# A fused attention and expert kernel: two more units take the two-level Strassen second product

## Chip, cores and metric

The kernel runs on one core of one Trainium2 chip. The metric is the device time of one execution in microseconds. The kernel before took a median of 1163.72 us in three runs (1161.91 to 1165.33).

A core has five engines that run side by side, each through its own instruction list in order: PE (matrix multiply), DVE (VectorE), ACT (ScalarE), POOL (GpSimd), and SP (SyncE), which here does nothing but issue transfers between DRAM and on-chip memory. An instruction that needs data from another engine, or a buffer that another still holds, waits on a semaphore at the head of its engine's list, and everything behind it in that list waits too.

## The reference

```
# 1. linear attention with decay, blocks of 64 positions
for b in range(nb):
    intra = ((qb @ kb.T) * Dmask) @ vb
    out[b] = intra + (qb * lam_pow) @ kv_state
    kv_state = lam_block * kv_state + (kb * rev_pow).T @ vb
# 2. bridge: (B,H,S,D) -> x of 3072 tokens x 512
# 3. mixture of 4 experts
p = probs / (probs.sum(-1) + 1e-9)
out = sum(p[:, e:e+1] * (relu(x @ w1[e]) @ w2[e]) for e in range(4))
```

There are 4 sequences, 8 heads, 768 positions and a head size of 64. Each w1[e] is 512 x 1024, each w2[e] is 1024 x 512. All is float32.

## The kernel before, in words

The 3072 tokens are cut into three groups of 1024 (g = 0, 1, 2). A **unit** is one group with one expert (g, e), so there are twelve; the list `units` has them in the order of the work. While the second product (h @ w2) of unit number `at` runs, the first product (x @ w1) of unit `at + 1` runs beside it, instruction by instruction.

**Strassen.** One Strassen level makes a product of 2 x 2 blocks with seven block products M1 to M7 instead of eight; its operands are blocks (A11, A12, A22) and sums of blocks (S1 to S4 of one factor, T1 to T4 of the other). The first product uses two levels in every unit: seven outer products, each of seven inner ones (`first_product`, matmuls in line 1017). The second product comes in two forms. Units 0 to `NEST - 1` use one level (`second_product`, line 1071): seven products, each summed into the tokens' accumulators and weighted with the gate by DVE (lines 1085 and 1089). Units from `NEST` on use two levels (`nested_product`, line 1370), and here `NEST` is 6: 4 operands of the outer level on the token side are made by DVE (`outer_sums`), 4 inner sums for each outer product by POOL (`inner_sums`, four 128 x 512 subtractions), the gate is multiplied onto the hidden values by POOL before the product (`gated`), and the result is collected in seven `sums` tiles, which occupy all seven buffers of the pool `stage`.

**Operands of w2.** The one-level form reads w2 blocks and the sums T1 to T4 of them (`prepare_w2`, stored in `w2_sums` in DRAM). The two-level form reads 49 operands for each expert, which POOL makes and SP stores in `w2_ops` in DRAM (`prepare_w2_ops`): blocks of w2 are loaded, four outer sums S1 to S4 are made (two 128 x 512 subtractions each), and for each of M1 to M7 four inner sums (four 128 x 256 subtractions) are made and stored in six transfers. The form called with `eased=True` uses tiles of the general pool `small` (42 buffers) instead of `stage`. The same kind of chain makes the operands of w1 (`prepare_w1`, stored in `w1_ops`).

**What sets the order of the work.** The order is written out by the Python code. A product is eight **slots** long; `now` counts slots. At the end of every slot `pump` may issue one preparation step from the list `chores`, if a count of the work given to POOL (`busy`) says that POOL is not behind. Finished sums are stored through `queue`, some slots later. Whoever needs an operand calls `until`, which, if the operand's store has not been issued, issues chores and stores one after another, at once, until it has been: `feed` (w1 operands, tile `ws_in`, line 930, two buffers, issued for the next product), `feed2` (one-level w2 operands, tile `w2t`, line 1052, two products ahead), `feed3` (two-level w2 operands, tile `w2t`, line 1129, six buffers shared with `feed2`; the first tile for a unit is fed in slot 1 of the last product before it). Gates, inner sums and DVE's work go through the lists `aside`, `background` and `lately`, one step a slot. All transfers named here are issued by SP, in the order of the code.

**Attention** of the groups 1 and 2 is woven into the units: `attention(g)` gives each of eight token blocks its load, transposes, scores and values at fixed slots, `BEGIN[g] = (first slot, slots from block to block)`. For each pair of blocks POOL makes block sums (`pair_sums`). `x_fill` loads the finished x of the group (tile `xs`) and POOL or DVE makes its inner sums.

**Before**, group 1 runs experts 0, 1 with one level and 2, 3 with two, and its one-level result goes through a DRAM buffer `partial` and is added at the end (`gather`, `finish_rows`). The w2 operands of experts 2 and 3 are made during units 4 and 5, those of experts 0 and 1 from unit 6 on, and the attention of group 2 runs from slot 152 to slot 276 (a unit has 56 slots).

Of the kernel before, what the change touches and what calls it, by code (L numbers as in the profile page):

```python
# [21 lines left out]
def kernel(  # L22
# [99 lines left out]
    units = [(g, e) for g in range(NG) for e in ((2, 3, 0, 1) if g == LAST else range(E))]  # L122
    unit_of = {u: x for x, u in enumerate(units)}
    NEST = 2 * E - 2
# [414 lines left out]
    gate_bc = decay[:]  # L539
# [240 lines left out]
    def pair_sums(g, x, o):  # L780

        s = stage.tile([P, 4, 256], FP32, name="to", tag="st")
        (b12, b11), (b22, b21) = ((t[:, 0:256], t[:, 256:512]) for t in o)
        for to, a, b in ((0, b12, b11), (1, b22, s[:, 0]), (2, b22, b12), (3, b21, s[:, 1])):
            tt(nc.gpsimd, s[:, to], a, b, ALU.subtract)
# [3 lines left out]
            nc.sync.dma_start(out=x_blocks[g - 1, :, x, 3:7], in_=s[:]),  # L789
# [4 lines left out]
    BEGIN = {1: (24, 13), 2: (8 * 19, 16)}  # L794
    steps = []

    def attention(g):
# [3 lines left out]

        for i in range(CPG):
            n, s = g * CPG + i, BEGIN[g][0] + BEGIN[g][1] * i
            put(s - 10, lambda n=n: load_more(n))
            put(s - 6, lambda n=n: load(n, "v"))
            put(s, lambda n=n: turn(n, ("s0", "s1")))
            if comes_across(n):
                put(s - 2, lambda n=n: (decayed(n), nat.pop((n, "k"))))
            put(s + (6 if comes_across(n) else 4), lambda n=n: scores(n, ("s0", "s1")))
            put(s + (12 if comes_across(n) else 10), lambda n=n: values(n, ("s0", "s1")))  # L810
            if n == NG * CPG - 1:
                put(s + 17, turn_gates)
        steps.sort(key=lambda s: s[0])

    def forget():
        while lately:
            take(lately, True)
        assert not states
# [38 lines left out]
    def gated(e, i, j, at, t):  # L857

        def step():
            n = j * 4 + (int(at[1]) - 1) * 2  # L860
            x = t[:].rearrange("p (c t) -> p c t", c=2)
            by = gate_bc[:, n:n + 2].rearrange("p n t -> p (n t)").unsqueeze(1).to_broadcast([P, 2, 256])
# [7 lines left out]
    def outer_sums(e, *names):  # L870
# [5 lines left out]
        def bring(x, at, tag):  # L876
# [3 lines left out]
            there[x] = bank(tag, "hp")  # L880
            nc.scalar.copy(out=there[x][:], in_=blk[at][:])  # L881

        def total(name, at):
            a, b = of[name]
            o = small("h" + name)
            tt(nc.vector, o[:], there[a][:], outer[e][b][at][:], ALU.subtract)
# [54 lines left out]
    def finished(g, e, m, blocks, new):  # L941

        def later(to, a, b, order, relu=False):
# [7 lines left out]
            def step(at):  # L951
                x = there[at]
                if unit_of[g, e] >= NEST and at != order[-1]:
# [11 lines left out]
            if unit_of[g, e] >= NEST:  # L965
# [90 lines left out]
    def second_product(g, e, m, banks):  # L1056

        def part(sj, s):
# [31 lines left out]
            if unit_of[g, e] in (E - 1, NEST - 1) and m in ("M2", "M6", "M5", "M3"):  # L1090
                to = rows[n] if g == 0 else partial[n % CPG * P:(n % CPG + 1) * P]
# [12 lines left out]
    partial = dram.tile([G, DOUT], FP32, name="partial")  # L1104
# [185 lines left out]
    def first_result():  # L1290
# [19 lines left out]
        def gather(n):  # L1310
            t, po = small("y"), small("po")
# [6 lines left out]
            nc.sync.dma_start(out=po[:], in_=partial[n * P:(n + 1) * P])  # L1318
            gathered_out[n] = t, po

        def turn_rows(n):
            t = gathered_out[n][0]
# [3 lines left out]
        def finish_rows(n):  # L1326
            t, po = gathered_out.pop(n)
            tt(nc.gpsimd, t[:], t[:], po[:], ALU.add)
            store(lambda: nc.sync.dma_start(out=rows[CPG + n], in_=t[:]))
# [296 lines left out]
    for g in range(1, NG):  # L1626
        attention(g)
    PACE = 1.0, 1.4, 1.0
    first_steps = first_result()
    PREPARED = {NEST - 2: (2, 3), NEST: (0, 1)}  # L1630
    for at, (g, e) in enumerate(units):
        if at == 0:
            chores.extend(prepare_w2(2) + prepare_w1(3) + prepare_w2(3) + prepare_w1(0))
        ahead = units[at + 1] if at + 1 < len(units) else None
        nested, nests = at >= NEST, ahead and at + 1 >= NEST
        if at in PREPARED:
            for x in PREPARED[at]:
                chores.extend(prepare_w2_ops(x, nested))
        if at == NEST:
            spare.append(True)  # L1640
        if at == NEST - 1:
            forget()
        blocks, banks = {}, {}
        for i in range(7):
# [8 lines left out]
            if nests and i == 2:  # L1653
                nc.scalar.dma_start(
                    out=gate_bc, in_=gate_rows[ahead[0] - 1, :, ahead[1]].partition_broadcast(P),
                )
# [24 lines left out]
            for x, part in enumerate(order):  # L1681
# [8 lines left out]
                elif (ahead or x % 2 == 0 and x + i) and not (nests and i == 6 and x == 7):  # L1690
                    if nested or nests:
                        rest()
# [60 lines left out]
```

## Time and profile before

| | |
|---|---|
| median of three runs | 1163.72 us |
| profiled execution, first to last instruction (span) | 1164.6 us |
| its own time as a run | not listed apart from the span |
| PE busy | 1149.6 us (99%) |
| POOL busy | 748.3 us (64%) |
| DVE busy | 810.8 us (70%) |
| ACT busy | 306.2 us (26%) |
| granted PE clock, mean | 0.998 |

In the page's groups a line such as `L1071 PE MATMUL q<-w2t,m` gives line, engine, operation, what is written and read, and then the number, the busy time and the mean time of one. One float32 matmul of the code leaves two records. Neighbouring matmuls overlap, so busy time divided by count, not the mean, is what one costs. A table of windows gives, for each stretch of the span, the busy time of each engine with its number of instructions, the granted PE clock, the share of busy transfer engines and the rate. The lines themselves are shown in the prediction.

### The profile page before, as it was taken

What the parts mean: (1) busy time and instruction counts of PE and PEld (TensorE: products, weight loads), DVE (VectorE), ACT (ScalarE), POOL (GpSimd) and SP (SyncE); (2) the same over time, 40 slices, a digit from 0 to 9 for tenths busy, and PEclk for the clock granted to TensorE, in tenths of its full rate; (3) what the DMA queues carried; (4) which work ended last, traced back from release to release, by engine and by line L of the source; (5) the groups of instructions that cost most, each with busy time, mean ns of one, the idle gap of its engine ahead of it and who ended that gap; (6) DMA issues with size and microseconds to landing.
All of it is one profiled execution on the core that took longest, in us unless ns stands there. A gap on an engine that the chain in (4) does not pass through costs nothing.

```text
span 1164.6 us, 21683 instructions
## 1 busy us (share of the span) xinstructions
PE 1149.6 (99%) x8039; PEld 997.4 (86%) x8039; DVE 810.8 (70%) x1483; ACT 306.2 (26%) x618; POOL 748.3 (64%) x720
## 2 busy tenths in 40 slices
PE   8899999999999999999999999999999999999998
PEld 7788888888888888888888888888888888888887
DVE  4576896477478757747946775688875677777785
ACT  4312122112201211221221243342343341341232
POOL 2747427456754862243646395897995898995894
PEclk9999999999999999999999999999999999999999
DMA  8883668999999797787969557676668877876542
GB/s 191 213 277 119 182 190 255 311 297 284 314 301 298 258 315 204 205 261 240 291 204 281 187 190 227 213 225 216 212 222 261 244 230 227 277 225 212 172 190 73
DMA packets 291705, 270.63 MB, mean 232 GB/s; under 512 B 139600, under 2 KB 239504, under 8 KB 291600
## 3 DMA queue, kind: packets, MB, share of 16 engines
q1 hardware_dynamic: 278848, 265.36, 74.1%
q10 hardware_dynamic: 12752, 3.89, 1.5%
q8 instruction: 64, 1.05, 0.4%
q14 instruction: 41, 0.34, 0.1%
HBM read 191.55 MB, written 81.82 MB: 235 GB/s over the span
## 4 chain that ended last, share of the span: by engine, by line
PE 93%; DVE 4%; DMA 1%; issue 1%; ACT 0%; ACTq 0%; DVEq 0%
PE pg L1017 39%; PE q L1071 24%; PE pq L1370 19%; PE pM L1473 3%; PE pc L1473 2%; DVE m L102 2%; PE sp L676 1%; PE op L730 1%; DMA ws_in<-w_ops 1%; PE op L748 1%; PE sp L683 1%; DVE sums L102 1%; PE qp L646 1%; PE kp L646 1%; DVE hT L102 0%
## 5 line engine op out<-in xcount | busy, mean ns | idle before, releaser
L1017 PE MATMUL pg<-xs,ws_in 128*128 128x256 f32 x1960 | 472.0, 381 | 2.3 <-DMA ws_in<-w_ops 1.2
L1017 PEld LDWEIGHTS pg<-xs,ws_in 128*128 128x128 f32 x1960 | 369.5, 190 | 56.5 <-DVE m L102 4.6
L102 DVE TENSOR_TENSOR m<-pg,m 128x512 f32<-128x512 f32 x451 | 307.1, 687 | 124.6 <-PE pg L1017 112.8
L1071 PE MATMUL q<-w2t,m 128*128 128x256 f32 x1344 | 318.7, 380 | 0.5 <-DVE m L102 0.5
L1071 PEld LDWEIGHTS q<-w2t,m 128*128 128x128 f32 x1344 | 254.1, 190 | 35.8 <-DVE m L102 1.2
L102 POOL TENSOR_TENSOR m<-m,decay 128x512 f32<-128x512 f32 x96 | 121.0, 1282 | 75.2 <-ACT m L1029 58.0
L1029 ACT ACTIVATE m<-m 128x512 f32<-128x512 f32 x132 | 83.0, 630 | 244.4 <-DVE m L102 241.0
L1370 PE MATMUL pq<-acc,w2t 128*128 128x256 f32 x576 | 141.9, 379 | 0.2 <-DVE sums L102 0.2
L102 DVE TENSOR_TENSOR sums<-pq,sums 128x256 f32<-128x256 f32 x223 | 92.7, 421 | 59.2 <-PE pq L1370 47.8
L1089 DVE SCALAR_TENSOR_TENSOR acc<-q,gate,acc 128x256 f32<-128x256 f32 x136 | 65.4, 481 | 87.5 <-PE q L1071 86.6
L1370 PEld LDWEIGHTS pq<-acc,w2t 128*128 128x128 f32 x576 | 109.2, 190 | 15.7 <-POOL w2o L102 0.5
L102 DVE TENSOR_TENSOR m<-m,m 128x512 f32<-128x512 f32 x136 | 112.9, 830 | 4.2 <-ACT m L1029 4.2
L1025 ACT COPY m<-pg 128x512 f32<-128x512 f32 x88 | 51.5, 585 | 161.7 <-PE pg L1017 158.7
L102 POOL TENSOR_TENSOR acc<-hT,acc 128x512 f32<-128x512 f32 x48 | 61.3, 1276 | 5.2 <-PE pq L1370 1.8
L102 POOL TENSOR_TENSOR to<-xc 128x256 f32<-128x256 f32 x16 | 12.6, 785 | 79.6 <-DVE xc L102 47.1
L102 POOL TENSOR_TENSOR acc<-hT,hT 128x512 f32<-128x512 f32 x48 | 60.7, 1282 | 3.9 <-PE pq L1370 3.9
L1370 PE MATMUL pq<-hT,w2t 128*128 128x256 f32 x240 | 61.6, 379 | 0.0
L102 POOL TENSOR_TENSOR xs<-xs 128x256 f32<-128x256 f32 x40 | 30.4, 761 | 47.0 <-DMA xs<-x_blocks 33.3
L102 POOL TENSOR_TENSOR kn<-kn,decay 128x512 f32<-128x512 f32 x16 | 18.1, 1133 | 63.2 <-PE kp L646 27.6
L949 ACT COPY up<-m 128x512 f32<-128x512 f32 x48 | 27.8, 589 | 101.6 <-DVE m L102 101.4
L881 ACT COPY hp<-m 128x512 f32<-128x512 f32 x72 | 41.6, 589 | 37.5 <-DVE hT L102 20.3
L1370 PEld LDWEIGHTS pq<-hT,w2t 128*128 128x128 f32 x240 | 45.6, 190 | 6.2
(140 smaller groups left out, 1371.0 us busy)
## 6 DMA issues: line engine op xcount, KB each, us to landing
ws_in<-w_ops SPq DMA_DIRECT2D x70, 896.0 KB, 6.9
w2t<-w_ops SPq DMA_DIRECT2D x108, 256.0 KB, 3.7
w2b<-in_moe_w_dram SPq DMA_DIRECT2D x56, 256.0 KB, 6.1
w_ops<-ops SPq DMA_DIRECT2D x28, 512.0 KB, 4.7
w2t<-w_sums SPq DMA_DIRECT2D x48, 256.0 KB, 3.7
w2t<-in_moe_w_dram SPq DMA_DIRECT2D x36, 256.0 KB, 3.9
w_sums<-w2o SPq DMA_DIRECT2D x16, 512.0 KB, 5.4
xs<-x_blocks SPq DMA_DIRECT2D x28, 256.0 KB, 4.5
```

What stands on the lines that cost most here:

```text
L102: eng.tensor_tensor(out=o, in0=a, in1=b, op=op)
L646: nc.tensor.transpose(out=x[:, ac * C:(ac + 1) * C], in_=y[:, 2 * ac:2 * ac + 2].rearrange("p r d -> p (r d)"), identity=ident[:],)
L676: nc.tensor.matmul(out=sp[r][half[x], ac * BL:(ac + 1) * BL], lhsT=hc(kT)[half[r], ac, blk[x]], rhs=hc(qT)[half[r], ac, blk[x]], start=(ac ...
L881: nc.scalar.copy(out=there[x][:], in_=blk[at][:])
L949: nc.scalar.copy(out=there[at][:], in_=a[at][:])
L1017: nc.tensor.matmul(out=p[:, j * 256:(j + 1) * 256], lhsT=ws[i][:, j * P:(j + 1) * P], rhs=xs[i], start=(fresh and j == 0), stop=True, skip ...
L1025: nc.scalar.copy(out=new[at][:], in_=p[:])
L1029: nc.scalar.activation(out=new[at][:], in_=new[at][:], func=AF.Relu)
L1071: nc.tensor.matmul(out=p[:, s * DH:(s + 1) * DH], lhsT=h[A_OF[m]][:, c * 256 + s * P:c * 256 + (s + 1) * P], rhs=fed2[g, e, m][uu][:, c], ...
L1089: nc.vector.scalar_tensor_tensor(out=o, in0=x, scalar=w, in1=o, op0=ALU.mult, op1=ALU.add)
L1370: nc.tensor.matmul(out=p[:, 0:256], lhsT=fed3[e, m, x // 2][:, x % 2, c * P:(c + 1) * P], rhs=b[B_OF[i]][:, c * 256:(c + 1) * 256], start= ...
L1473: nc.tensor.matmul(out=p[:, s * 256:(s + 1) * 256], lhsT=a[c][:, f:f + P], rhs=b[:, c, j * 256:(j + 1) * 256], start=(s == 0 and c == 0 an ...
```

## The change

`NEST` becomes 4, so units 4 and 5 use the two-level form too; group 1 now runs its experts in the order 2, 3, 0, 1, like group 2. The buffer `partial` and its addition are gone. The two-level operands of w2 for experts 2 and 3 are made by chores of the units 0 to 3; whatever is left of `chores` when unit 4 begins is issued there at once. Those of experts 0 and 1 are listed as chores at the start of unit 4. The attention of group 2 starts at slot 128 with 13 slots from block to block and ends in unit 4. Each two-level unit gets its own pair of gate tiles (`spread_gates`) in place of the shared one. In unit 4 the outer sums and some additions read on-chip tiles directly, without the copy to PSUM that later units use (`unit_of[g, e] > NEST`).

```diff
-    units = [(g, e) for g in range(NG) for e in ((2, 3, 0, 1) if g == LAST else range(E))]
+    units = [(g, e) for g in range(NG) for e in ((2, 3, 0, 1) if g else range(E))]
...
-    NEST = 2 * E - 2
+    NEST = E
...
+    def spread_gates(g, e):
+        gate_bc[unit_of[g, e]] = two = [small("gb")[:].rearrange("p (n t) -> p n t", t=P) for _ in range(2)]
+        for j, t in enumerate(two):
+            src = gate_rows[g - 1, 4 * j:4 * j + 4, e]
+            nc.scalar.dma_start(out=t, in_=src.partition_broadcast(P))
...
-        s = stage.tile([P, 4, 256], FP32, name="to", tag="st")
+        s = [small("to") for _ in range(2)]
...
-    BEGIN = {1: (24, 13), 2: (8 * 19, 16)}
+    BEGIN = {1: (24, 13), 2: (24 + 8 * 13, 13)}
...
+        def idle(slot):
+            return ("s0", "s1") if slot < NEST * 56 else (("q11", "q12"), ("q01", "q02"))[slot // 8 % 2]
...
-            there[x] = bank(tag, "hp")
-            nc.scalar.copy(out=there[x][:], in_=blk[at][:])
+            if e > NEST:
+                there[x] = bank(tag, "hp")
+                nc.scalar.copy(out=there[x][:], in_=blk[at][:])
...
-            t, po = gathered_out.pop(n)
-            tt(nc.gpsimd, t[:], t[:], po[:], ALU.add)
-            store(lambda: nc.sync.dma_start(out=rows[CPG + n], in_=t[:]))
+            t = gathered_out.pop(n)
+            nc.sync.dma_start(out=rows[CPG + n], in_=t[:])
...
-    PREPARED = {NEST - 2: (2, 3), NEST: (0, 1)}
...
-            chores.extend(prepare_w2(2) + prepare_w1(3) + prepare_w2(3) + prepare_w1(0))
+            chores.extend(
+                prepare_w2(2) + prepare_w1(3) + prepare_w2_ops(2, False) + prepare_w2(3) + prepare_w2_ops(3, False)
+                + prepare_w1(0)
+            )
...
-        if at in PREPARED:
-            for x in PREPARED[at]:
-                chores.extend(prepare_w2_ops(x, nested))
         if at == NEST:
+            while chores:
+                print("forced")
+                pump(force=True)
+            for x in (0, 1):
+                chores.extend(prepare_w2_ops(x, True))
             spare.append(True)
...
-                nc.scalar.dma_start(
-                    out=gate_bc, in_=gate_rows[ahead[0] - 1, :, ahead[1]].partition_broadcast(P),
-                )
+                spread_gates(*ahead)
```

## Prediction

> **What bounds the kernel now.** I read the page's busy times first, then a table of windows by unit, then what one instruction and one transfer cost, and last the piece of the chain where PE once had to wait. From the page:
>
> ```profile
> span 1164.6 us, 21683 instructions
> PE 1149.6 (99%) x8039; PEld 997.4 (86%) x8039; DVE 810.8 (70%) x1483; ACT 306.2 (26%) x618; POOL 748.3 (64%) x720
> ```
>
> PE is busy almost throughout, so a matmul less shortens the run, provided that nothing makes PE wait. The windows (window; busy us and instructions of PE, PEld, DVE, ACT, POOL; clock; transfer share; GB/s) show a start-up stretch, unit 4 (one level, attention beside it), unit 5 (one level), and units 7 to 10 (two levels); the bounds are where the second product's line or unit changes in the timeline.
>
> ```profile
> 44.00:48.00 4.00, 3.95 (x62) 3.78 (x62) 2.30 (x4) 0.92 (x2) 3.62 (x4) 0.57 0.76 233
> 495.00:594.60 99.60, 99.60 (x838) 86.32 (x836) 70.37 (x126) 17.82 (x40) 45.43 (x52) 1.00 0.85 258
> 594.60:686.30 91.70, 91.15 (x422) 79.55 (x421) 59.14 (x94) 21.91 (x38) 55.32 (x54) 1.00 0.66 207
> 767.20:850.90 83.70, 83.61 (x388) 73.16 (x387) 70.57 (x129) 27.52 (x49) 73.01 (x65) 1.00 0.71 222
> 850.90:935.60 84.70, 82.88 (x379) 71.29 (x378) 54.15 (x94) 35.99 (x75) 67.17 (x60) 1.00 0.77 241
> 935.60:1017.30 81.70, 81.70 (x379) 71.72 (x378) 61.28 (x113) 25.20 (x45) 74.12 (x70) 1.00 0.80 244
> 1017.30:1099.90 82.60, 82.60 (x384) 72.55 (x384) 61.38 (x115) 24.42 (x43) 64.00 (x53) 1.00 0.70 213
> ```
>
> Seen here: a one-level unit takes 91.7 us, 99.6 with attention; a two-level one takes 83.2 (mean of four), 11.9 per outer product, 1.49 per slot. POOL is at 64 to 74 us of such a unit: near its limit, but PE doesn't wait, because the preparation is spread evenly. Prices, from the groups and the transfer list (the last figure is us to landing):
>
> ```profile
> L102 POOL TENSOR_TENSOR acc<-hT,hT 128x512 f32<-128x512 f32 x48 | 60.7, 1282 | 3.9 <-PE pq L1370 3.9
> L102 POOL TENSOR_TENSOR ops<-w2o 128x256 f32<-128x256 f32 x28 | 20.7, 760 | 0.2
> ...
> ws_in<-w_ops SPq DMA_DIRECT2D x70, 896.0 KB, 6.9
> w2t<-w_ops SPq DMA_DIRECT2D x108, 256.0 KB, 3.7
> w2b<-in_moe_w_dram SPq DMA_DIRECT2D x56, 256.0 KB, 6.1
> w_ops<-ops SPq DMA_DIRECT2D x28, 512.0 KB, 4.7
> ...
> L315 SPq DMA_DIRECT2D w_ops<-ops x84: 319/496/2052, 513.3 to 1052.6; - x84
> ```
>
> So POOL takes 1.28 us for a 128x512 subtraction and 0.76 for a 128x256 one; issuing a transfer holds SP 0.5 us. Last, the chain:
>
> ```profile
> 883.80 1.51 PE pg L1017 x7
> 885.31 11.68 DMA ws_in<-w_ops
> 896.99 0.14 issue
> 897.13 1.97 PE pg L1017 x8
> ```
>
> The first product's weights are issued about one product (11.9 us) ahead and arrive just in time. Whatever holds SP for longer stops PE.
>
> **The change part by part.**
>
> *Gain.* 91.7 - 83.2 = 8.5 us a unit, 17 for two. Counted otherwise: 28 records fewer a unit, at 318.7/1344 = 0.237 us, 13.3 for two. I take 15.
>
> *Added POOL work, by count.* 32 more gate products and 56 more inner subtractions, 8 additions fewer: 80 x 1.28 = 102 us. In all, 748 + 102 = 850 of some 1150 us fits. What matters is when it comes. The order that the changed code builds shows four places where chores are not spread but issued together, because a reader forces them or because unit 4 begins. After unit 4's start the count of POOL's work is 40 slots ahead, so `pump` issues nothing until unit 5 ends; the operands for experts 0 and 1 are then made only when `feed3` asks.
>
> *A, start of unit 4.* In the last four products of unit 3 POOL is given 16.3, 12.3, 21.0 and 15.4 us of work (instructions by the rows) against 99.6/7 = 14.2 us each, so it is 8.1 late. Then eleven steps of expert 0's w1 chain stand at once in POOL's and SP's lists; SP gets to the `w2t` loads of unit 4's first product only behind the store of the tenth. Ten steps: six times 4 x 0.76 and four times 2 x 1.28, 28.5 us, and 3 for block A12, whose load (7.8 us to landing, w1b 512 KB) stands behind the third store. 8.1 + 31.5 + 3 issues 1.5 + load 3.7 = 44.8. PE needs the tile in slot 4 with some scores before it, 6.5 us in. Stall 38. Without lateness and A12: 27; with 12 of lateness and 5 of waits for the seven `stage` buffers: 48.
>
> *B, expert 0's operands.* In slot 1 of unit 5's last product ten steps are forced. One gate product and four leftover block sums of attention hold POOL, and SP behind them, for 4.6 us; two stores and four loads issue (3.0); landing 6.1: 13.7. S1 2.6, four sums for M4 3.0, S3 2.6, four for M7 3.0, four for M1 3.0: 27.9. Six stores issue (3.0), then the first `w2t` can load, its pieces having landed by 32.6: 36.3. Due after 7 slots, 10.4: stall 26. `ws_in` issues behind it at 33.6 and lands at 40.5, while PE has 1.5 us to do: 3 more. In the next product M3's operands are forced: after M1 POOL has M5 (3.0), nine 128x512 (11.5), then S2, M6, M2, S4, M3 (14.2), done at 56.6; landing 4.7, load 3.7 and issues 1.5: 66.5. PE is through at 40.5 + 10.4 = 50.9: stall 15.6, and 2.5 again for `ws_in`. B = 47; from 30 (stores and loads half hidden) to 55.
>
> *C, expert 1's, one unit later.* The same without block sums and first loads, but behind twelve sums of x (9.1): M1 ready on POOL at 1.3 + 9.1 + 14.2 = 24.6 in place of 27.9. C = 47 - 3.3, rounded 43; from 27 to 52.
>
> *D, units 2 to 3.* The T3 and T4 of expert 3 are forced too. Loads 3 + 6.1, sum 2.6, store 5.4 (w_sums 512 KB), then two `w2t` and one `ws_in` issue and land, 1.5 + 6.9: 25.5 against a due time of 16, a stall of 9.5 for T3 and less for T4, whose blocks are partly there. I take 10; from 0 to 20.
>
> *Clock.* In the window 44 to 48 the clock is 0.57 after an idle of 2.49 us: (1 - 0.57) x 4 = 1.7 us lost. Five long stalls (A, B twice, C twice): 8.5; none to nine (also the 2.5 us ones): 0 to 15. The Trainium skill (TensorE: Matmul & The Clock Gate, Part 1) puts the drop to half speed after an idle window of about 3.4 us; the trace's gap was shorter, so by the row the short second waits count too (15), by the page they don't (8.5).
>
> *At nothing.* The removed `partial` traffic (24 transfers, 8 additions) lay beside PE, and SP waited little there. Ten more gate transfers on ACT's queue: ACT is busy 26%. Seven inner sums and gates a unit: POOL would have 56 us of 83 in a unit without chores. Denser attention: the same instructions, earlier; DVE at 70 of 99.6 in unit 4 covers it, else it is the second rival.
>
> Sum: -15 + 38 + 47 + 43 + 10 + 8.5 = +131.5; 1164.6 + 131.5 = 1296. The profiled execution is 0.9 above the median: 1295.
>
> One more weighing. The trace has 3.7 to 6.9 us per landing. The skill (DMA: Bandwidth & Descriptors, section Anatomy of one DMA) gives 2.0 us plus size over 436 GB/s, 2.6 for 256 KB and 4.1 for 896 KB; by it each of the four chains in B and C would be some 8 us shorter, and the sum 1263. The row decides, as transfer engines are 66 to 85% taken here. The same page says that a wait for a semaphore happens on the issuing sequencer, which speaks against queuing stores of unfinished sums ahead of loads.
>
> **Rivals.**
>
> 1. *The bursts are absorbed, faster.* Between 740 and 840 us POOL was busy 88.84 of 100 us and PE still 99.91. If A, B, C, D end before their due times, the gain remains: 1164.6 - 15 - 1 = 1149. It decides where a chain is below 6.5 us (A) or 10.4 (B, C). Against: POOL's work alone is 28.5 and 14.2, and can't start earlier than SP and POOL reach it.
>
> 2. *DVE becomes the bound.* Attention of group 2 comes every 13 slots instead of 16, beside unit 4's outer sums, which now read two on-chip tiles (0.83 against 0.68 us). Units 3 and 4 each lose 15 to DVE and the bursts cost nothing: 1164.6 - 15 + 30 = 1180. Against: DVE has 70 of 99.6 us.
>
> 3. *Half the chains hide.* POOL and SP run ahead while PE stands, so the second waits of B and C (18 each) and D vanish and A takes its low end: 1164.6 - 15 + 27 + 29 + 25 + 5 - 1 = 1235, down to 1215.
>
> 4. *The chains lengthen each other*: stores crowd the transfer engines, all upper ends: -13 + 48 + 55 + 52 + 20 + 15 = +177, 1341 and above.
>
> **How the numbers follow.** Main case 0.66; rival 1 0.05; rival 2 0.05; rival 3 0.14; rival 4 0.10. The low ends of the main case give -17 + 27 + 30 + 27 = +67, 1231. The range 1215 to 1345 takes in rival 3 and the main case; outside remain 1 and 2 and about half of 4. No change can be told apart below 0.3%, 3.5 us: faster 0.05, same 0.01, slower 0.94.
>
> **What would show it.** Right: PE's idle time in five or six gaps of 13 us or more, at the first product of unit 4 and at the ends of units 5 and 6, ended by `w2t` or `ws_in` transfers; SP waiting for POOL's `ops`; POOL full there and under 70% in units 8 to 10; a clock below 1 after each; L1071 at 896 records. Wrong: gaps ended by DVE, or no gap. My sum would be too high if POOL reaches the forced steps before PE reaches their place, too low if buffers of `small` or `stage` come free late.

## The result, and the profile after

The changed kernel takes 1357.02 us (median of four runs, 1354.96 to 1358.48) against 1163.83: a ratio of 1.166, 95% interval [1.164, 1.168]. The profiled execution has a span of 1356.0 us, 191.4 more than that of before. The forecast was 1295, from 1215 to 1345: the sign is right, the time lies 62 us above the number and 12 above the range.

Lines move with the change: the first product is now L1027, the one-level second product L1081, the two-level one L1376, its copies by ACT into `sums` L1384, the copies `hp` L891, the load of `ws_in` L940, of a two-level `w2t` L1138. From the page of the changed kernel, span and PE:

```profile
span 1356.0 us, 21829 instructions
PE 1176.8 (87%) x7983; PEld 1009.3 (74%) x7983; DVE 836.1 (62%) x1525; ACT 316.4 (23%) x638; POOL 861.3 (64%) x800
```

The records fall by 56, as counted. Yet PE is busy for 27 us longer, and between its first and its last instruction it stands for 174.2 us where it stood 10.4. The busy time holds two opposite things. Laying the clock records of the trace beside PE's busy time, PE ran 71.5 us at half clock (granted clock 0.5; before: 3.4), which lost 35.7 us (1.7). What is left, the work at full clock, is 1141.1 us against 1147.9. So 191.4 is 163.8 more of standing and 34.0 more of half clock, less 6.8 of work: 191.0. The other 0.4 us lie behind PE's last instruction.

Where PE stands, by windows of the changed kernel (window; busy us and instructions of PE, PEld, DVE, ACT, POOL; clock; transfer share; GB/s):

```profile
380.00:480.00 100.00, 75.37 (x629) 62.35 (x627) 46.62 (x83) 12.22 (x26) 41.00 (x45) 0.88 0.73 212
480.00:570.00 90.00, 61.72 (x468) 51.78 (x468) 45.76 (x75) 10.52 (x25) 73.27 (x75) 0.87 0.82 252
570.00:640.00 70.00, 38.97 (x240) 32.19 (x241) 27.27 (x39) 10.76 (x25) 55.04 (x53) 0.71 0.50 170
640.00:790.00 150.00, 143.36 (x653) 125.36 (x652) 93.97 (x166) 42.54 (x82) 87.00 (x71) 0.98 0.51 159
790.00:900.00 110.00, 75.72 (x326) 65.12 (x325) 54.43 (x99) 22.24 (x39) 81.28 (x77) 0.83 0.69 217
900.00:990.00 90.00, 53.82 (x218) 44.63 (x217) 40.34 (x73) 17.62 (x31) 75.42 (x77) 0.77 0.55 181
990.00:1150.00 160.00, 158.50 (x727) 136.81 (x726) 117.75 (x208) 61.61 (x121) 107.56 (x84) 1.00 0.55 175
```

The first two rows are the end of unit 2 and unit 3, the place of D: 52.9 us idle. The third is A, the start of unit 4: 31.0. The fifth and sixth are B and C: 34.3 and 36.2. After 990 all is as before. What ended PE's longer waits, from the list of waits (us in total, times, longest):

```profile
PE pq L1376 <- DVE sums L102: 39.1, 5, 19.2
PE pq L1376 <- DMA w2t<-w_ops: 28.4, 3, 15.5
PE pg L1027 <- DMA ws_in<-w_ops: 25.0, 4, 13.6
PE pq L1376 <- ACT sums L1384: 22.5, 1, 22.5
PE pg L1027 <- DVE m L102: 12.6, 8, 6.4
PE pg L1027 <- issue: 12.1, 1, 12.1
PE op L736 <- DVE kv L102: 11.4, 6, 5.3
```

Transfers of `w2t` and `ws_in` end 53 us of it, but the largest row is DVE. How a burst on POOL comes to look like a wait for DVE shows in the timeline of the changed kernel at B (start, duration, engine, line, operation; in brackets the idle time before and what ended it):

```profile
789.61 2.49 POOL L102 TENSOR_TENSOR w2o<-w2b 128x512 f32<-128x512 f32 x2 [6.41 <-DMA w2b<-in_moe_w_dram]
...
806.36 2.49 POOL L102 TENSOR_TENSOR m<-m,gb 128x512 f32<-128x512 f32 x2
...
807.65 0.59 ACT L891 COPY hp<-m 128x512 f32<-128x512 f32 x1 [26.09 <-POOL m L102]
...
808.27 0.69 DVE L102 TENSOR_TENSOR hT<-hp,m 128x512 f32<-128x512 f32 x1 [20.46 <-ACT hp L891]
808.88 0.75 DVE L102 TENSOR_TENSOR sums<-pq,sums 128x256 f32<-128x256 f32 x2
...
809.35 2.08 PE L1376 MATMUL pq<-hT,w2t 128*128 128x256 f32 x4 [18.82 <-DVE sums L102]
...
841.91 2.08 PE L1376 MATMUL pq<-m,w2t 128*128 128x256 f32 x4 [15.47 <-DMA w2t<-w_ops]
```

POOL is given the forced steps first and the gate product `m<-m,gb` behind them, at 806.4. ACT's list stands at the copy of that gated tile, DVE's at the sum that reads the copy, and behind it in DVE's list wait the additions that empty PE's banks. So PE stops as soon as the burst begins, in the middle of a product whose own operands are all there. The second gap, 15.5 us, is the `w2t` load of the next product.

At A the chain of waits of the changed kernel, up to the matmul that ends the 22.5 us:

```profile
574.88 2.28 POOL ops L102 x2
...
590.90 4.95 DMA w1b<-in_moe_w_dram
...
599.00 2.46 DMA w_ops<-ops
601.46 0.37 ACT sums L1384
...
601.87 2.50 PE pq L1376 x5
```

That is the forced chain on POOL, as in the prediction, with the load of block A12 in it. Its last link is another one: ACT's first copy into a `sums` tile waits until the `stage` buffer that it takes has been stored. The `w2t` tile then costs only 0.7 us. The load of A12, priced at 3 us, cost POOL next to nothing: in this stretch POOL stands for 0.4 us at most.

The 12.1 us that the list puts down to "issue" are none of the four places. The changed kernel's timeline of SP, and of PE, near 480 us:

```profile
457.12 9.95 SPq L441 DMA_DIRECT2D across<-in_q_dram  x11
467.11 10.41 SPq L441 DMA_DIRECT2D across<-in_k_dram  x16
...
485.23 0.41 SPq L940 DMA_DIRECT2D ws_in<-w_ops  x1
...
491.97 3.75 PE L1027 MATMUL pg<-xs,ws_in 128*128 128x256 f32 x8 [12.05 <-issue]
```

Attention of group 2 reads q and k from `across`, a buffer in DRAM which `trickle` fills with one small transfer at every odd slot. `load_more` issues whatever pieces are still missing. Attention now comes earlier, so 27 pieces are missing; SP issues them in 20 us, with `ws_in` behind them.

### The profile page after: what moved, and what is told of

Its sections match the earlier page's. It is cut to its first block, busy times and chain, and to the rows that moved or that the text cites. A ratio compares the mean times of both kernels' runs of the same rounds, so it can differ in the third digit from the quotient of the medians.

```text
span 1356.0 us, 21829 instructions
## 1 busy us (share of the span) xinstructions
PE 1176.8 (87%) x7983; PEld 1009.3 (74%) x7983; DVE 836.1 (62%) x1525; ACT 316.4 (23%) x638; POOL 861.3 (64%) x800
## 4 chain that ended last, share of the span: by engine, by line
PE 67%; POOL 11%; DMA 8%; DVE 6%; SPq 5%; issue 3%; ACT 0%; ACTq 0%; POOLq 0%; DVEq 0%
PE pg L1027 28%; PE pq L1376 20%; PE q L1081 11%; POOL ops L102 4%; DMA ws_in<-w_ops 3%; DVE m L102 2%; POOL acc L102 2%; POOL m L102 2%; PE pc L1479 2%; PE pM L1479 1%; DVE hT L102 1%; DVE sums L102 1%; SPq L441 1%; SPq L158 1%; POOL w2o L102 1%
## 5 line engine op out<-in xcount | busy, mean ns | idle before, releaser
L1027 PE MATMUL pg<-xs,ws_in 128*128 128x256 f32 x1960 | 486.1, 389 | 49.7 <-DMA ws_in<-w_ops 25.0
L1027 PEld LDWEIGHTS pg<-xs,ws_in 128*128 128x128 f32 x1960 | 379.5, 195 | 110.1 <-issue 38.3
L102 POOL TENSOR_TENSOR m<-m,gb 128x512 f32<-128x512 f32 x128 | 167.4, 1322 | 127.0 <-ACT m L1039 80.8
L1376 PE MATMUL pq<-acc,w2t 128*128 128x256 f32 x800 | 205.4, 391 | 30.0 <-ACT sums L1384 22.5
L102 DVE TENSOR_TENSOR sums<-pq,sums 128x256 f32<-128x256 f32 x321 | 133.4, 421 | 151.8 <-PE pq L1376 106.3
L1081 PE MATMUL q<-w2t,m 128*128 128x256 f32 x896 | 218.2, 387 | 1.3 <-DVE m L102 1.3
L1376 PEld LDWEIGHTS pq<-acc,w2t 128*128 128x128 f32 x800 | 157.0, 197 | 54.5 <-ACT sums L1384 22.7
L1081 PEld LDWEIGHTS q<-w2t,m 128*128 128x128 f32 x896 | 172.6, 194 | 26.7 <-DVE m L102 1.7
L1376 PE MATMUL pq<-hT,w2t 128*128 128x256 f32 x336 | 88.4, 386 | 38.1 <-DVE sums L102 38.0
L1376 PEld LDWEIGHTS pq<-hT,w2t 128*128 128x128 f32 x336 | 64.6, 193 | 48.1 <-DVE sums L102 39.3
L1376 PE MATMUL pq<-m,w2t 128*128 128x256 f32 x264 | 73.0, 402 | 29.3 <-DMA w2t<-w_ops 27.6
L102 DVE TENSOR_TENSOR m<-m,m 128x512 f32<-128x512 f32 x96 | 81.2, 846 | 5.1 <-DMA x_blocks<-xc 3.0
L1376 PEld LDWEIGHTS pq<-m,w2t 128*128 128x128 f32 x264 | 52.3, 201 | 39.3 <-DMA w2t<-w_ops 28.4
L891 ACT COPY hp<-m 128x512 f32<-128x512 f32 x84 | 47.9, 589 | 89.4 <-POOL m L102 73.0
L102 DVE TENSOR_TENSOR hT<-hp,m 128x512 f32<-128x512 f32 x56 | 38.1, 680 | 43.8 <-ACT hp L891 43.8
```

Of the source, the lines that this page charges most:

```text
L102: eng.tensor_tensor(out=o, in0=a, in1=b, op=op)
L1027: nc.tensor.matmul(out=p[:, j * 256:(j + 1) * 256], lhsT=ws[i][:, j * P:(j + 1) * P], rhs=xs[i], start=(fresh and j == 0), stop=True, skip ...
L1081: nc.tensor.matmul(out=p[:, s * DH:(s + 1) * DH], lhsT=h[A_OF[m]][:, c * 256 + s * P:c * 256 + (s + 1) * P], rhs=fed2[g, e, m][uu][:, c], ...
L1376: nc.tensor.matmul(out=p[:, 0:256], lhsT=fed3[e, m, x // 2][:, x % 2, c * P:(c + 1) * P], rhs=b[B_OF[i]][:, c * 256:(c + 1) * 256], start= ...
```

## The experiments

### Bursts of forced steps

First, the count that keeps the steps of experts 0 and 1 back until `feed3` asks is set back.

```diff
 while chores:
     pump(force=True)
+busy[0] = free[0] = now[0]
```

> The changed kernel; after the steps forced at the start of unit 4 the count of POOL's work and the time of the next step are set back to now, so that w2 operands of experts 0 and 1 are issued one by one through units 4 to 6 and not when `feed3` asks. In the order that this builds, the ten steps forced at the end of unit 5 become none, the six after them one, and expert 1's eleven and six become five and six. My theory (a burst costs what PE waits for its chain, and a clock loss behind it): the 70.5 us that PE idles between 800 and 990 us become about 20, with 11 us of clock loss there mostly gone: 1357 - 50 - 8 = 1299, from 1275 to 1315. The rival (POOL has no room in units 4 to 6, so the same work only makes other things late): 1340 or more.

Measured: 1295.4 us, ratio to before 1.113 [1.110, 1.116], 61.7 below the changed kernel and inside the theory's range. The trace has 52.0 us less of standing and 8.8 less of half clock. The gaps of 18.8 and 15.5 us at B are gone; of C's 19.2, 12.2 and 4.3 there remain 7.6, 11.5 and 3.6, where eleven steps are still forced. The work is the same and POOL has room for it; the cost was in its coming all at once.

The reverse, one burst put into the kernel before:

```diff
+held = {}
 def until(what):
+    chores.extend(held.pop(what[:2], ()))
...
-    chores.extend(prepare_w2_ops(x, nested))
+    if x == 0:
+        held["w2", x] = prepare_w2_ops(x, nested)
+    else:
+        chores.extend(prepare_w2_ops(x, nested))
```

> The kernel before; the steps that make expert 0's w2 operands are kept back until `feed3` asks for them at the end of unit 9, and nothing else is changed: one burst by itself (nine steps, then six), without the attention, the backlog and the other bursts of the changed kernel. Theory: it costs what expert 1's burst costs in the changed kernel, 36 us of idle and 5 to 8 of clock loss: 1163.7 + 42 = 1206, from 1190 to 1215. Rival (a burst costs much only where POOL is late already): up to 1178.

Measured: 1197.8, ratio 1.028 [1.026, 1.031], so +34 for one burst of 15 steps, inside the theory's range. The timeline of PE shows the same pair of gaps as at B, with the same releasers:

```profile
1041.06 2.07 PE L1373 MATMUL pq<-hT,w2t 128*128 128x256 f32 x4 [16.47 <-DVE sums L102]
...
1067.96 2.07 PE L1373 MATMUL pq<-m,w2t 128*128 128x256 f32 x4 [9.86 <-DMA w2t<-w_ops]
```

So B and C need nothing else of the changed kernel to happen. Next, in this kernel, the link from POOL to ACT was cut by giving unit 10's gate products to DVE:

```diff
-tt(nc.gpsimd, x, x, by, ALU.mult)
+tt(nc.vector if e == 10 else nc.gpsimd, x, x, by, ALU.mult)
```

> The run with one burst in the kernel before, and the sixteen gate products of unit 10 on DVE in place of POOL, so that ACT's copy and with it DVE's list no longer wait behind the burst. Theory 1 (the two gaps, 16.5 and 9.9 us, are one chain: what PE gains at the first it waits longer for the `w2t` tile of the second, which comes when POOL's list of the second burst is done): 1192, from 1187 to 1198. Theory 2 (they are two waits, each for itself): the first goes, 1197.8 - 16.5 = 1181 or less.

Measured: 1192.0, ratio 1.024 [1.023, 1.026]. The number is that of theory 1, the way there is neither theory's. From the timeline of PE:

```profile
1034.05 2.05 PE L1373 MATMUL pq<-m,w2t 128*128 128x256 f32 x4 [5.58 <-DMA w2t<-w_ops]
...
1059.11 2.07 PE L1373 MATMUL pq<-m,w2t 128*128 128x256 f32 x4 [5.08 <-DMA w2t<-w_ops]
```

The first gap falls from 16.5 to 5.6, which shows that the gate products behind the burst made most of it; what is left is a wait for `w2t`, the kind of wait that the prediction expected. The second does not grow; it falls from 9.9 to 5.1. The edit also takes sixteen products off POOL's list, so how much of the second fall is due to that stays open. Standing is 12.4 us less in all, but five short gaps (2.2, 5.6, 2.4, 5.1, 2.1) lose 9.9 us to half clock where gaps of 16.5, 9.9 and 2.4 lost 6.2, and the full-clock work is 1.4 longer: 7.3 us in the profiled runs, 5.9 in the medians. One of the five, 2.2, belongs to the start-up, 1000 us earlier, and its 1.7 us of half clock have nothing to do with the edit.

### The place of attention

```diff
 if x % 2:
-    trickle()
+    trickle(2)
```

> The changed kernel; `trickle` moves two small pieces of q and k to `across` at each odd slot in place of one, so that `load_more` finds none left when the third group's attention, which now starts earlier, wants them. Theory: the stall that is seen between 480 and 530 us (18.1 us of idle, and half clock behind it) is SP issuing some thirty small transfers in one go ahead of `ws_in` and `x_blocks`; it goes away: 1357 - 18 - 5 = 1334, from 1328 to 1342. Rival (the stall is the rest of the T3 and T4 chain, and the pieces only stand beside it): 1352 to 1362.

Measured: 1348.6, ratio 1.157 [1.155, 1.160], 8.4 less: between the two. The gap of 12.1 is gone, and gaps over 3 us fall from 146.4 to 129.1 us together, but shorter ones grow by 10.2; the pieces cost something at their new places too. The other half of the test, attention's new place alone in the kernel before:

```diff
-BEGIN = {1: (24, 13), 2: (8 * 19, 16)}
+BEGIN = {1: (24, 13), 2: (24 + 8 * 13, 13)}
```

> The kernel before with only the places of the third group's attention as in the changed kernel: from slot 128, every 13 slots. Theory: it costs the pieces of `across`, which were worth 8.4 us in the changed kernel, and little beside: 1172, from 1164 to 1180. Rival (denser attention makes DVE the bound for two units): 1190 or more.

Measured: 1182.0, ratio 1.015 [1.013, 1.017], +19, just outside the theory's range. It is one gap. SP and PE of this run:

```profile
437.72 10.88 SPq L441 DMA_DIRECT2D across<-in_k_dram  x16
...
453.33 0.47 SPq L930 DMA_DIRECT2D ws_in<-w_ops  x1
...
460.44 3.75 PE L1017 MATMUL pg<-xs,ws_in 128*128 128x256 f32 x8 [15.37 <-DMA ws_in<-w_ops]
```

DVE, the rival, stops PE nowhere for more than two microseconds (1.7 at most). What the earlier attention costs by itself is SP's list.

### The spacing of the first four units

```diff
-PACE = 1.0, 1.4, 1.0
+PACE = 0.8, 1.4, 1.0
```

> The changed kernel; the steps of preparation in the first four units are issued with 0.8 of their counted spacing in place of 1.0. In the order that this builds, nothing is forced for T3 and T4 of expert 3, no step is left to force at the start of unit 4, and of expert 0's operands four steps in place of ten are forced at the end of unit 5; expert 1's stay as they are. Theory: idle at 404 to 445 us (20 us) and at 602 us (22.5 us) goes, with some 12 us of clock loss, and B loses 5 to 15: 1357 - 65 = 1292, from 1275 to 1310. Rival (POOL and the transfer engines, 93 to 95% taken from 200 to 380 us, can't go faster, so the waits only move): 1340 or more.

Measured: 1313.9, ratio 1.128 [1.124, 1.131], 43.1 less, where 65 was expected, and so between the theory and the rival. The gaps for T3 and T4 and A's 22.5 are gone. In their place stand one of 21.9 us at the pieces of `across` (12.1 before), and one of 17.2 us at the start of unit 4, put down to DVE: there POOL has expert 0's last w1 steps, attention's decays and unit 4's gate products at once, and DVE's list stands for 17.4 us at sums that need a gated tile.

All together, with steps 5 instead of 7 slots apart from unit 4 on, at a spacing of 0.75 and of 0.65:

> The changed kernel with all of it together: the spacing of the first four units at 0.75, the count set back at the start of unit 4, two pieces per odd slot, and steps no closer than 5 slots in place of 7 from unit 4 on, so that only four steps are still forced (expert 1's last). Theory (the costs of the places add): 1357 less 61.7 (count set back), 8.4 (pieces), 43.1 (spacing) is 1243.8; the rest of C, two gaps of 19 us together and 4 of clock, goes too, as do some of the 21.9 us that the pieces cost once the spacing was shorter: 1215, from 1200 to 1240. Rival (POOL and the transfers have no room, the waits move on): 1255 or more.

> The same with the spacing of the first four units at 0.65, so that POOL has no step of preparation left from the second product of unit 3 on, in place of the fifth. Theory (with 0.8 a 17.2 us gap at the start of unit 4 was left, where gate products stood in POOL's list behind the last w1 steps): it goes, 10 to 20 us below the run at 0.75. Rival (transfer engines, 93 to 95% taken from 200 to 380 us, set the pace there): as long as the run at 0.75, or longer.

Measured: 1259.4, ratio 1.082 [1.080, 1.084], and 1266.9, ratio 1.089 [1.087, 1.091]. The rival has both: the gains don't add. At 0.75 PE stands 23 us from 200 to 400 us, where it stood 4.3 in the changed kernel. From the windows of this run:

```profile
200.00:300.00 100.00, 88.92 (x811) 75.44 (x810) 61.52 (x106) 17.57 (x41) 59.83 (x61) 0.95 0.89 269
300.00:400.00 100.00, 88.08 (x783) 73.81 (x784) 52.63 (x93) 13.01 (x30) 55.57 (x63) 0.93 0.89 272
400.00:500.00 100.00, 82.95 (x671) 69.49 (x671) 55.73 (x93) 14.50 (x32) 67.27 (x78) 0.90 0.93 283
```

POOL is free for about a third of each row or more, the transfer engines are taken to 0.89 and more, and from 200 to 620 us `ws_in` ends 30.8 us of PE's waits. But full transfer engines alone do not explain it. In the kernel before they were taken to 0.95 there, and PE hardly stood:

```profile
200.00:300.00 100.00, 99.92 (x1001) 86.34 (x1001) 67.94 (x124) 20.92 (x49) 58.81 (x64) 1.00 0.95 293
300.00:400.00 100.00, 99.45 (x697) 86.21 (x696) 67.97 (x114) 18.60 (x36) 60.39 (x63) 1.00 0.95 301
```

In the three longest of these waits (5.8, 7.0 and 8.5 us) SP issued the load only 2.2 and 0.9 us before PE came to stand for it, and 0.1 us after; ahead of it SP had issued other stores and loads one after another. The last of the three:

```profile
477.83 0.54 SPq L940 DMA_DIRECT2D ws_in<-w_ops  x1
...
486.24 3.75 PE L1027 MATMUL pg<-xs,ws_in 128*128 128x256 f32 x8 [8.51 <-DMA ws_in<-w_ops]
```

The three landed after 7.8, 7.8 and 8.3 us, where the median of the kernel before is 6.9. So in these waits the place in SP's list counted for more than the speed of the transfer; the shorter ones were not taken apart.

At 0.65 there is a gap of 16.5 us, in the timelines of POOL and PE of that run:

```profile
336.01 2.49 POOL L102 TENSOR_TENSOR w2o<-w2o,w2b 128x512 f32<-128x512 f32 x2 [10.89 <-DMA w_ops<-ops]
...
353.19 1.06 POOL L102 TENSOR_TENSOR kn<-kn,decay 128x512 f32<-128x512 f32 x1
...
354.30 1.13 PE L689 MATMUL sp<-vn,kn 64*64 64x64 f32 x32 [16.50 <-POOL kn L102]
```

POOL itself stands 10.9 us, for a store that still holds the buffer of its next sum, and attention's decay of k comes behind it. Steps of preparation are transfers too; issued sooner, they wait for their own stores and stand ahead of the loads in SP's list.

### The change without its preparation

To see what is left when nothing is forced, all two-level units read expert 2's operands, and the others' are not made. The edit of the changed kernel, which also moves two pieces of `across` per odd slot (in the kernel before, the first two lines and `PREPARED = {NEST - 2: (2,)}` do the same):

```diff
-x_e = units[e][1]
+x_e = 2
...
-prepare_w2(2) + prepare_w1(3) + prepare_w2_ops(2, False) + prepare_w2(3) + prepare_w2_ops(3, False)
+prepare_w2(2) + prepare_w1(3) + prepare_w2_ops(2, False) + prepare_w2(3)
...
-for x in (0, 1):
-    chores.extend(prepare_w2_ops(x, True))
...
-trickle()
+trickle(2)
```

> The kernel before with one set of w2 operands: all two-level units read expert 2's, and those of experts 0, 1 and 3 are not made, so three of four experts' second products there are computed with the wrong weights. Theory: PE waits for nothing in the kernel before, so less preparation saves nothing: 1160 to 1164. Rival (preparation slows PE even where no wait is seen, by the transfers that it takes): below 1158.

> The changed kernel with one set of w2 operands in the same way (three experts' second products wrong), and two pieces per odd slot. A, B and C are gone with the work; the steps for T3 and T4 of expert 3 are still forced (five and four). Theory: what stays is the pure gain, 7 us (the trace has 1141.1 us of PE work at full clock in place of 1147.9), and D's T3 and T4 chains, in the run with two pieces per slot gaps of 9.9 and 6.5 us with 5 us of clock loss: 1163 - 7 + 21 = 1177, from 1168 to 1190. Rival (attention of the third group, 13 slots apart, and DVE cost two units 15 us each): 1190 or more.

> The same with the spacing of the first four units at 0.8, so that no step is forced at all: the two-level units without any burst. Theory: the pure gain and two small gaps as seen with that spacing (7.5 us, 4 of clock): 1163 - 7 + 11 = 1167, from 1154 to 1172. Rival 1 (the gain is 15 and bursts were all that stood against it): 1150 or less. Rival 2 (work that is spread costs as well, by transfers): 1180 or more.

Measured: the kernel before 1163.4, ratio 1.000 [0.999, 1.001], as expected: preparing the operands of three experts costs it nothing. The changed one 1227.3, ratio 1.055 [1.054, 1.057], and with the spacing of 0.8 1213.4, ratio 1.044 [1.042, 1.046]. Here my theory fell, and the rivals of 1190 or more and 1180 or more have the numbers: without one forced step the change still costs 50 us. Between the profiled runs (1162.0 and 1215.3) that is 45.3 more of standing and 16.5 of half clock, less 8.8 of work. The standing is spread over gaps of at most 8.4 us from 200 to 600 us. In the run at the old spacing, 11.1 us from 480 to 620 us are waits for `kv`, the running state of attention that DVE sums up:

```profile
PE op L736 <- DVE kv L102: 11.1, 6, 3.3
```

They lead to a part of the change that the prediction did not price and that the diff above leaves out: in unit 3 and from there on, `lately`, the list of attention's DVE work, is taken only if `fits()` finds room. Sixteen pieces are left until the next piece of attention forces them, with PE at that place. Two edits, apart and together:

```diff
-if lately and fits():
+if lately:
...
-prepare_w2(2) + prepare_w1(3) + prepare_w2_ops(2, False) + prepare_w2(3)
+prepare_w2(2) + prepare_w1(3) + prepare_w2(3) + prepare_w2_ops(2, False)
```

> The run with one set of w2 operands (three experts' second products wrong), and in the slots of unit 3 and of the two-level units the attention's waiting DVE work (`lately`) is taken in every slot, not only where the count finds room on DVE (`fits`). In the order that this builds, none of it is left to be forced by the next piece of attention; without the edit sixteen pieces are. Theory (the idle time from 500 to 600 us, 18.3 us in gaps up to 3.4, with 9.2 of clock loss, is PE waiting for attention's sums that were left too late): it goes, 1227 - 24 = 1203, from 1198 to 1212. Rival (DVE is too full there, and the banks of the products wait instead): 1220 or more.

> The run with one set of w2 operands, and the w2 sums of expert 3 made ahead of expert 2's inner operands; nothing is forced for T3 and T4 any more, and the spacing is the changed kernel's. Theory (the gaps of 14.5 and 7.1 us between 400 and 450 us are the forced T3 and T4): they go with some 4 of clock, 1227 - 25 = 1202, from 1197 to 1210. Rival (transfer engines, 98% taken from 380 to 450 us, are late there anyway): 1218 or more.

> Both of these edits on the run with one set of w2 operands. Theory (apart places, costs add): 1227 - 24 - 25 = 1178, from 1170 to 1188. Rival (with the pauses gone, transfers or POOL come late in their place): 1195 or more.

Measured: the w2 sums first, 1203.2, ratio 1.034 [1.031, 1.036], 24.1 less, as expected: the forced T3 and T4 alone are worth that. `lately` in every slot, 1216.5, ratio 1.046 [1.043, 1.048], 10.8 less instead of 24. Both, 1200.7, ratio 1.031 [1.029, 1.034], as the rival had it: beside the first edit, `lately` gives only 2.6, which is within the noise. The waits of this run from 480 to 620 us say why:

```profile
PE pg L1027 <- DVE m L102: 19.1, 2, 18.6
...
DVE hT L102 <- POOL m L102: 18.2, 2, 10.6
```

The waits for `kv` are gone, and a new one has come: as with the spacing of 0.8, DVE's list stands at a gated tile that POOL has not come to. So the steps were brought to an earlier end, by a spacing of 0.85 beside both edits:

> The run with one set of w2 operands (three experts' second products wrong), the w2 sums of expert 3 first and `lately` in every slot, with the spacing of the first four units at 0.85: POOL's last step of preparation then comes in product 3 of unit 3, ahead of most gate products of unit 4's operands. Theory (the 18.6 us gap at 515 us is POOL with the last w1 steps, attention's decays and unit 4's gate products and inner sums all at once, while DVE's list stands at a sum that needs a gated tile): it goes, 1200.7 - 20 = 1181, from 1172 to 1188. Rival (the steps that come earlier make `ws_in` and attention's loads late between 200 and 400 us by as much): 1195 or more.

Measured: 1186.4, ratio 1.020 [1.017, 1.023], 14.3 less, as the theory had it; the gap of 18.6 is gone. What remains between 1163.4 and 1186.4 was not taken apart further: the profiled run (span 1179.9) stands 11.4 us from 200 to 300 us, mostly where attention waits for POOL's decay of k (11.7 us in all), and loses 6.4 us to half clock.

### The clock

```diff
+if x == 0 and m == "M3" and e in (6, 7):
+    for _ in range(50):
+        nc.tensor.matmul(out=p[:, 0:P], lhsT=ident[:], rhs=ident[:], start=True, stop=True)
```

> The changed kernel with 50 products of the unit matrix with itself (128x128) on PE ahead of the first matmul of the outer product M3 of units 6 and 7, where PE stands 15.5 and 12.2 us for a `w2t` tile; their result is overwritten. Theory (the clock is halved because PE stood still): PE has work for some 11 us of each wait, the clock stays full or falls only for one record, and of the 2.1 and 4.1 us that were lost there some 4 come back: 1353, from 1350 to 1356. Rival (the halving comes from elsewhere, such as the load of the other engines): the records show half clock at both places all the same, and the time is 1357 or more.

Measured: 1356.5, ratio 1.165 [1.162, 1.167], no difference from the changed kernel and half a microsecond outside the theory's range. The windows at the two places, first of the changed kernel, then of this run:

```profile
824.00:849.00 25.00, 9.53 (x35) 7.75 (x34) 5.87 (x11) 2.99 (x6) 21.67 (x22) 0.66 0.86 280
949.00:977.00 28.00, 11.54 (x34) 8.68 (x33) 5.61 (x10) 3.35 (x6) 22.34 (x22) 0.63 0.71 239
```

```profile
824.00:849.00 25.00, 20.20 (x135) 18.59 (x134) 5.79 (x11) 2.89 (x6) 21.62 (x22) 0.93 0.84 274
949.00:977.00 28.00, 22.15 (x138) 19.97 (x137) 6.33 (x11) 3.36 (x6) 22.60 (x22) 0.88 0.71 239
```

With PE at work the clock is 0.93 and 0.88 in place of 0.66 and 0.63: it is PE's standing that halves it. Yet the time did not follow. The waits for `w2t` (15.5 and 12.2 us) become 4.8 us and none, and right after the second PE waits 5.5 us for `ws_in` (4.3 before). After the first PE goes on at 842.4 us, in the changed kernel at 841.9; after the second at 970.8 and 971.4. POOL's and SP's chains end when they ended, so a PE that is not slowed only waits for the next tile. Not all of the 34 us of half clock is time that would come back.

### The best of these versions

> The run with the count set back, two pieces per slot and the spacing at 0.75 (all operands made), and `lately` taken in every slot. Theory: of its 17.9 us of idle and 5.4 of clock loss from 500 to 600 us most goes: 1259 - 18 = 1241, from 1234 to 1248. Rival (there it is POOL's backlog that holds DVE): 1253 or more.

> The changed kernel, all operands made, with all the edits: count set back, two pieces per slot, spacing 0.75 and from unit 4 on 5 slots, `lately` in every slot, the w2 sums of expert 3 first. Theory (w2 sums first take away nothing more, since at 0.75 T3 and T4 were not forced; the rest is late transfers from 200 to 500 us): 1250, from 1238 to 1256, and no version of this kind comes near the kernel before. Rival (each edit still counts): 1235 or less.

Measured: 1253.3, ratio 1.076 [1.074, 1.078], and with the w2 sums of expert 3 first as well 1242.0, ratio 1.069 [1.066, 1.071]. The first gave 6 where 18 was expected. The second lies in its theory's range, 8 below its number, but by luck: the theory said that the w2 sums first would take away nothing more, and they took 11.3. The last is the best version with all operands made, 115 us below the changed kernel and 79 above the kernel before. None of these versions beats the kernel before.

## Why the prediction was right and wrong

**Right: the sign and its main cause.** Forced steps stop PE, at the four places that the prediction names, and little elsewhere after 640 us. The kernel with one burst added shows the mechanism alone (+34 for one burst), setting the count back shows it the other way (-61.7). By the prediction's own signs the result is mixed: of five gaps of 13 us or more, two were ended by transfers (15.5 and 13.6), two by DVE (19.2 and 18.8), which it names as a sign of being wrong, and one by ACT (22.5).

**A (38, from 27).** The gap was 22.5 us, the window of A 31.0 idle with the 5.3 us wait for `kv` that follows. So the window lies within the term's range (27 to 48) and the gap alone below it. It is the forced chain on POOL, but it ended in a `stage` buffer for `sums`, not in a `w2t` tile, and A12's load, 3 us in the sum, was hidden. (The upper end adds up to 47, not 48, and C's middle to 43.7.)

**B and C (47 and 43).** Measured 34.3 and 36.2: both within their ranges (30 to 55 and 27 to 52), but well below the middle. The step that failed is the place of the first stall. The prediction lets PE go on for 10.4 us, to the end of the product, and then wait for `w2t`. PE stopped at once, since DVE waited for ACT and ACT for a gate product behind the burst, and the first `w2t` tiles of the next unit were issued at 805.3, in the shadow of this stall. With the gate products off POOL (one burst in the kernel before), the expected wait for `w2t` did appear, with 5.6 us. The prediction counted the gate product only as something that holds POOL and did not ask who waits for it.

**D (10, from 0 to 20).** This is the term that failed most: 52.9 us idle. T3 and T4 alone, sized at 9.5 and less, were gaps of 13.6 and 6.8, and worth 24.1 us when they were taken away. The other 32 us or so of standing have causes that the prediction does not have, or costs "at nothing": the pieces of `across` in front of `ws_in` on SP (a gap of 12.1; +19 for attention's place in the kernel before), `lately` taken only where `fits()` allows, and POOL's full list at the end of unit 3. The last two were tested only in other versions (one set of operands, a shorter spacing); how the shorter gaps of the changed kernel divide between them stays open. For "denser attention" the prediction named DVE's share of 70 in 99.6 us as cover. DVE was the cover for DVE's work; the transfers that attention issues had none.

**Clock (8.5, from 0 to 15).** 34.0 us. The 1.7 us per stall came from one short gap in the start-up; here a stretch at half clock loses 1.7 to 4.2 us, 2.6 on average, and in place of five stalls there were 14 such stretches. The Trainium skill (TensorE: Matmul & The Clock Gate, Part 1) puts half speed after at least one idle window of about 3.4 us, and says that the window runs freely. The stretches here do come in multiples of 3.4 us, but in the changed kernel a gap of 2.1 us was followed by one, a gap of 2.5 us was not, and one stretch (at 389 us) came with gaps of 0.7 and 1.3 us alone. The measurement decides: a gap shorter than the window can cost it. The prediction took the page's side (8.5) and kept the row's as its upper end (15); both were far too low, since they counted too few stalls and too little for each.

**Gain (15).** 6.8 us in the changed kernel, 8.8 in the pair without preparation. The record count (56) was right, the price of one was not: 0.237 us is L1071's busy time divided by its count, but the two products run interleaved, and their overlapping parts are counted in both lines. With each instant given to the matmul that started last, a record of the second product takes 0.219 us in the kernel before, and 56 are 12.3 us. By the same count the second product of the changed kernel takes 10.2 us less at full clock, and the other matmuls, equal in number, 3.3 us more. Why they take longer stays open; that matmuls next to a gap lose their overlap was not tested.

**The other weighing.** The 1263 that the prediction sets beside its sum uses the fit of "Anatomy of one DMA", which the page gives for transfers issued by gpsimd; those here are issued by SP.

**Rivals.** 1 (absorbed) and 3 (half the chains hide) are refuted. 2 (DVE is the bound, 1180) is refuted as a time, but DVE's list as the place where PE is held is real, at B, C and in unit 3. The result lies where rival 4 put it (1341 and above), but not for its reason: A, B and C were all below their middle.

In the terms of the sum, measured against predicted: work -6.8 (-15), D 52.9 (10), A 31.0 (38), B 34.3 (47), C 36.2 (43), other places 9.4 (0), clock 34.0 (8.5): 191.0 against 131.5. A, B and C were priced 26.5 too high together, and by luck this hid part of the 86 by which the other terms were too low.

## What to carry to other kernels

When work is moved in a kernel whose engines run their lists in order, ask of every instruction that lands behind a burst who waits for it, and of every list it passes what else it holds: here PE stood for DVE, which stood for ACT, which stood for POOL, and SP's small attention transfers delayed the weights. Spreading the forced steps, with the other edits beside it, won back 115 of 193 us and not more, because waits that went let others show, on the lists of DVE and POOL and on SP's list of transfers. What the transfer engines, nine tenths taken there, add to it was not shown. A planner's count that runs ahead (40 slots here) is itself a cause: look for the place where it stops issuing, not only for the place where it is forced.

## What was not expected of the hardware

- Half clock comes more by the number of gaps than by their length: a gap of 22.5 us lost 2.7 us, one of 2.1 us lost 1.7, in stretches of 3.4 us and multiples. Four gaps of 2.1 to 5.6 us around a burst lost 8.2 us together, three of 16.5, 9.9 and 2.4 lost 6.2.
- A small transfer holds SP longer in a row than the 0.5 us of a large one alone: 16 pieces of `across` took 10.4 and 10.9 us to issue, 0.65 to 0.68 each.
- Landing times fell although the kernel moved a little more (273.0 MB, before 270.6, but over a longer span: 201 GB/s against 232): 2.9 us for `w2t<-w_ops` where before had 3.7, 4.7 for `w2b` where it had 6.1, while `ws_in` stayed (6.8 and 6.9). The Trainium skill (DMA: Bandwidth & Descriptors, section Anatomy of one DMA) would give 2.6 for the first two, of 256 KB, and 4.1 for the last, of 896 KB: close for the first alone. Its fit is for transfers issued by gpsimd, and these are issued by SP. Its sentence that a wait is made on the issuing sequencer agrees with the trace, where SP stood 44.1 us at the stores of `ops` for POOL.
